# Spreading q and k by DMA and transposing them in 32x32 blocks on VectorE instead of TensorE

## The chip, the cores and the metric

One Trainium2 chip, one of its cores. The metric is the device time of one execution of the program in microseconds; lower is better. The profile is that of one execution, and its times are counted from the first instruction of the program (the start of the span).

## The reference

Chunked attention over eight batches of eight heads (576 rows, head size 64, chunks of 64 rows that attend only to themselves), and behind it a low-rank mix of the rows and a two-layer MLP with a residual:

```python
q_c = q.reshape(B, H, nc, chunk, D)        # B=8, H=8, S=576, D=64, chunk=64, nc=9
scores = scale * np.matmul(q_c, k_c.transpose(0, 1, 2, 4, 3))
scores = scores - np.max(scores, axis=-1, keepdims=True)
attn = np.exp(scores)
attn = attn / (np.sum(attn, axis=-1, keepdims=True) + 1e-09)
out = np.matmul(attn, v_c)
...
x = out.transpose(0, 2, 1, 3).reshape(B, S, H * D)   # 8 x 576 x 512
h = xt @ U @ V                                       # xt: x with the last two axes swapped, rank 32
u = x + h.transpose(0, 2, 1)
return u + np.maximum(u @ w_ch1, 0.0) @ w_ch2        # 512 -> 2048 -> 512
```

q, k, v are float32; U, V and the two weight matrices are float64 and are converted on the chip.

## The kernel before

The batches are worked in four pairs. A pair has 1152 rows, which are nine tiles of 128 rows; the tiles are named (pair, tile), (0,0) to (3,8). Three tiles make a group of 384 rows, on which the MLP works. Tile 4 of each pair straddles the two batches, so its loads come in two segments.

**Attention of one tile** (`attention_ops`). `load_qk` (L376) brings q and k of 128 rows with rows on partitions and heads and head elements along the free axis (256-byte pieces, one DMA each for q and k per segment, on SP's queue), `load_v` (L392) brings v in four DMAs. TensorE then turns q (`ps_qT`) and k (`ps_kT`): four 128x128 transposes each (L419) into a PSUM bank, which ScalarE copies to SBUF (`evacuate`, L433) as `qT_` and `kT_`. So head pairs stand side by side: heads 2h and 2h+1 fill the two halves of the partitions. The scores are 32 matmuls of 64x64 (L441), VectorE takes maxima and subtracts (L455, L459), ScalarE exponentiates (L463), TensorE transposes the result (`ps_eT`, L419 again), ScalarE copies it, 32 matmuls multiply with v (L472), VectorE scales into the tile's `x` (L490).

**MLP block** (one group, one f of 16): twelve matmuls of 384 columns `h` (L638), ScalarE's relu `hh` (L646), VectorE's remainder `hl` (L651), nine matmuls of 512 columns `o` (L664). TensorE sends the `o` matmuls of one block behind the `h` matmuls of the next, so relu and remainder have the time of one `h` and one `o` stretch. There are 192 blocks, 12 groups by 16.

**The weights** arrive during the first 190 us: for each f one `wraw` load (L325 and L329, 512 KB each, on SP), then a conversion from float64 that begins with ScalarE's L86 (`magnitude`), goes through six VectorE instructions and ends with ScalarE's L348 and VectorE's L351. ScalarE and VectorE run their instructions in order, relu and conversion on one queue.

**Order of the work.** All of pair 0's tiles ("early"), the weights, the first 32 MLP blocks (groups 0 and 1 of pair 0, both taking each f in turn as its weights arrive, `STRETCHES`) and tiles (1,0) and (1,1) (placed behind blocks 28 and 30, `GATES`) are `Op`s with an engine, a cost in us and the SBUF slots and PSUM banks that they take and free; `order()` simulates them and fixes the order on each engine. Behind that, pairs 1 to 3 run through `plan()`: during the 16 blocks of a group, the attention steps of coming tiles (`attend`), the low-rank steps and the mixing are laid between the MLP's matmuls at even distances, and the framework's scheduler settles the order. `attend` calls `ahead` at the start of a tile, which loads the next tile. q, k, v, their transposes and other temporaries of pairs 1 to 3 share eight `slot` buffers.

SP's queue issues, in order, nearly all DMAs: weights, q, k, v of pairs 1 to 3, and the stores of the output (L679).

Of the kernel before, what the change touches and what calls it, by code (L numbers as in the profile page):

```python
# [10 lines left out]
F32 = mybir.dt.float32  # L11
# [10 lines left out]
def kernel(  # L22
# [11 lines left out]
    nc = tc.nc  # L34
    B, H, S, D = q.shape
# [3 lines left out]
    DF, DM = moe_w_ch2.shape[0], moe_w_ch1.shape[0]  # L39
    P = 128  # L40
    C = 64
    D1 = D + 1
    HP = H // 2
    NCC = DM // P
    NF = DF // P
    NT = 2 * S // P
    GT = 3
    NEARLY = 9
    NX = 10
# [5 lines left out]
    NPAIR = B // 2  # L55
# [5 lines left out]
    work = ctx.enter_context(tc.tile_pool(name="work", bufs=1))  # L61
    psum = ctx.enter_context(tc.tile_pool(name="psum", bufs=8, space=bass.MemoryType.PSUM))

    dram = ctx.enter_context(tc.tile_pool(name="dram", bufs=1, space=bass.MemoryType.DRAM))
# [4 lines left out]
    def slot(dtype, name, shape=(P, 512)):  # L69
        return work.tile(list(shape), dtype, tag="slot", name=name, bufs=NS)  # L70
# [40 lines left out]
    rank = [0]  # L111
# [248 lines left out]
    def segments(pr, t):  # L360
        lo, hi = t * P, (t + 1) * P
        for e in range(2):
            a, z = max(lo, e * S), min(hi, (e + 1) * S)
            if a < z:
                yield a - lo, z - a, 2 * pr + e, a - e * S

    def early(pr, t):
        return pr == 0 and t < NEARLY

    loaded = {}  # L370
    begun = {}
    x_of = {}
    y_of = {}
    ut_of = {}

    def load_qk(pr, t):  # L376
        n = f"{pr}_{t}"
        if early(pr, t):
            words = wslot((4 * DM,), F32, "qkv_" + n)
            qn, kn = (words[:, z * DM : (z + 1) * DM].rearrange("p (h d) -> p h d", h=H) for z in range(2))  # L380
            vn = words[:, 2 * DM : 2 * DM + H * D1].rearrange("p (c a k) -> p c a k", c=2, k=D1)
        else:
            qn = slot(F32, "qn_" + n, (P, H, D))
            kn = slot(F32, "kn_" + n, (P, H, D))
            vn = slot(F32, "vn_" + n, (P, 2, HP, D1))
        nc.gpsimd.memset(vn[:, :, :, D:], 1.0)  # L386
        for r, m, b, s0 in segments(pr, t):
            nc.sync.dma_start(qn[r : r + m], q[b, :, s0 : s0 + m, :].rearrange("h s d -> s h d"))
            nc.sync.dma_start(kn[r : r + m], k[b, :, s0 : s0 + m, :].rearrange("h s d -> s h d"))
        loaded[pr, t] = qn, kn, vn  # L390

    def load_v(pr, t, behind=None):  # L392
        vn = loaded[pr, t][2]
        for c in range(2):
            b, s0 = divmod(t * P + c * C, S)
            b += 2 * pr
            for e in range(2):
                queue = nc.gpsimd if early(pr, t) else nc.sync
                d = queue.dma_start(
                    vn[e * C : (e + 1) * C, c, :, 0:D],  # L400
                    v[b, e::2, s0 : s0 + C, :].rearrange("h s d -> s h d"),
                )
                if behind is not None and c == e == 0:
                    sync = mybir.DependencyInfo(mybir.DependencyClass.Sync, mybir.DependencyReason.DATA)
                    tc.add_manual_dep(d.ins, behind.ins.name, sync, reason="q and k go first")

    def load(pr, t):
        load_qk(pr, t)
        load_v(pr, t)

    def attention_ops(pr, t, after=None):
        n = f"{pr}_{t}"
        st = {}
        mine = early(pr, t)

        def transpose(src, name):
            ps = st[name] = bank("ps_" + name + n)
            for j in range(4):
                o = nc.tensor.transpose(  # L419
                    ps[:, j * P : (j + 1) * P], src[:, j * P : (j + 1) * P], ident  # L420
                )
            if mine and name == "qT_":
                q_last[t] = o

        def evacuate(name):
            if name[0] == "e" or not mine:
                dst = slot(F32, name + n, (P, HP, P))
            elif name[0] == "q":
                st["qk"] = wslot((2, HP, P), F32, "qkT_" + n)
                dst = st["qk"][:, 0]  # L430
            else:
                dst = st["qk"][:, 1]
            nc.scalar.copy(dst.rearrange("p a b -> p (a b)"), st[name])  # L433
            st[name] = dst
# [51 lines left out]

        def scaled(e):
            if e == 0:
                st["x"] = work.tile([P, HP, 2, D], F32, tag="x", name="x_" + n, bufs=NX)
            nc.vector.tensor_mul(  # L490
                st["x"][:, :, e, :],
                st["av"][e][:, :, 0:D],
                st["sm"][:, e].unsqueeze(2).broadcast_to([P, HP, D]),
            )
            if e == 1:
                x_of[pr, t] = st["x"].rearrange("p a b k -> p (a b k)")

        src = lambda z: loaded[pr, t][z].rearrange("p h d -> p (h d)")
        flat = lambda: st["ex"].rearrange("p a b k -> p (a b k)")
        lq = Op("SP", 3.4, lambda: load_qk(pr, t), after, take="w" if mine else "slot slot slot", lat=1.6)  # L500
        tq = Op("PE", 0.55, lambda: transpose(src(0), "qT_"), lq, begun.get((pr, t - 2)), take="bank")
        lv = Op(
            "POOL" if mine else "SP",
            2.5,
# [2 lines left out]
            lat=2.2,  # L507
        )
        if mine:
            tqs[t], lvs[t] = tq, lv  # L510
        cq = Op("ACT", 0.58, lambda: evacuate("qT_"), tq, take="w" if mine else "slot", free="bank")
        tk = Op("PE", 0.55, lambda: transpose(src(1), "kT_"), lq, tq, take="bank")
        ck = Op("ACT", 0.58, lambda: evacuate("kT_"), tk, cq, take="" if mine else "slot", free="bank")
        sc = Op("PE", 0.62, scores, ck, take="bank bank", free="w" if mine else "slot slot slot slot")
        m0 = Op("DVE", 0.41, lambda: maximum(0), sc, take="slot mx")
        s0 = Op("DVE", 0.41, lambda: subtract(0), m0, free="bank")
        m1 = Op("DVE", 0.41, lambda: maximum(1), s0)
        s1 = Op("DVE", 0.41, lambda: subtract(1), m1, free="bank mx")
        ex = Op("ACT", 0.63, exp, s1)
        te = Op("PE", 0.55, lambda: transpose(flat(), "eT_"), ex, take="bank", free="slot")  # L520
        ce = Op("ACT", 0.58, lambda: evacuate("eT_"), te, take="slot", free="bank")
        av = Op("PE", 0.65, values, ce, lv, take="bank bank x", free="slot w" if mine else "slot slot")
        sm = Op("DVE", 0.5, sums, av, take="sm")
        x0 = Op("DVE", 0.415, lambda: scaled(0), sm, free="bank")
        x1 = Op("DVE", 0.415, lambda: scaled(1), x0, free="bank sm")
        begun[pr, t] = te
        return [[lq, lv], [tq, cq], [tk, ck], [sc, m0, s0, m1, s1, ex], [te, ce], [av, sm, x0, x1]]

    ybank = {}
    q_last, tqs, lvs, ahead = {}, {}, {}, {}  # L530
# [187 lines left out]
    WORK = "U T3 T4 T8 T5 T2 T1 T7 T0 T6 W0 P0 P1 V M0 M1 W1 W2 W3 W4 W5 W6 W7 W8 W9 W10 W11 W12 W13 W14 W15".split()  # L718
    STRETCHES = ((0, 0, 2), (1, 0, 2), (0, 2, 3), (1, 2, 3), (0, 3, 4), (1, 3, 4), (0, 4, 5), (1, 4, 5), (0, 5, 6), (1, 5, 6), (0, 6, 7), (1, 6, 7), (0, 7, 8), (1, 7, 8), (0, 8, 9), (1, 8, 9), (0, 9, 10), (1, 9, 10), (0, 10, 11), (1, 10, 11), (0, 11, 12), (1, 11, 12), (0, 12, 13), (1, 12, 13), (0, 13, 14), (1, 13, 14), (0, 14, 16), (1, 14, 16))
    GATES = (28, 30)  # L720
    BASE = 1000
    u_done = None
    v_done = []
# [5 lines left out]
    for item in WORK:  # L729
        rank[0] += 1  # L730
        begin = len(ops)
        z, i = item[0], int(item[1:] or 0)
# [21 lines left out]
        lvs[b].after.append(tqs[a])  # L754
    prev = None
    blocks = 0
    gates = dict(zip(GATES, range(len(GATES))))
    for g, f0, f1 in STRETCHES:
        for f in range(f0, f1):
            rank[0] = BASE  # L760
            prev = block_ops(0, g, f, f == 0, f == NF - 1, [*w_done[f], *mixed[g]], prev)
            blocks += 1
            if (g, f) == (0, NF - 1):
                last = prev
            if blocks in gates:
                rank[0] = 0
                attention_ops(1, gates[blocks], prev[0])
    assert blocks == 2 * NF
    rank[0] = 0
    for t in range(6, NT):  # L770
# [19 lines left out]
    manual.__exit__(None, None, None)  # L790


    tiles = [(pr, t) for pr in range(NPAIR) for t in range(NT)]
    pend = None

# [10 lines left out]
    def attend(ts):  # L806
        steps = []
        prev = None
        for key in ts:
            i = tiles.index(key)  # L810
            _, q, k, sc, et, av = attention_ops(*key)

            def ahead(i=i):
                if i + 1 < len(tiles) and tiles[i + 1] not in loaded:
                    load(*tiles[i + 1])

            steps += [ahead, step(*q)] + ([prev[0]] if prev else [])
            steps += [step(*k)] + ([prev[1]] if prev else []) + [step(*sc)]
            prev = step(*et), step(*av)
        return steps + (list(prev) if prev else [])  # L820
# [72 lines left out]
```

## Time and profile before

| | |
|---|---|
| runs | 1003.51, 1002.9, 1005.02 us; median 1003.51 us |
| span of the profiled execution | 1000.9 us; its page gives no other time of this execution |
| TensorE matmuls (PE) | 980.2 us busy, 98% |
| TensorE weight loads (PEld) | 854.2 us, 85% |
| VectorE (DVE) | 405.6 us, 41% |
| ScalarE (ACT) | 256.9 us, 26% |
| SP's DMA queue | 120320 packets, 52.18 MB, 20.5% of the time of 16 DMA engines |

In the profile a line such as `L419` is a line of the kernel; `<-` names what an instruction writes and reads; `x4` counts instructions. In rows of groups the numbers after the bar are busy time in us, mean time of one instruction in ns, and the idle time of the engine just before them with the instruction that ended it. Matmuls are pipelined and their ends are modelled: two that follow each other overlap, so the distance from start to start, not the duration, is what one adds to TensorE's time. In the timeline the first two columns are start and duration in us, several alike instructions are merged into one row, and square brackets give the idle time before. SP's rows are issues of DMAs.

### The profile page before, as it was taken

What the parts mean: (1) busy time and instruction counts of PE and PEld (TensorE: products, weight loads), DVE (VectorE), ACT (ScalarE), POOL (GpSimd) and SP (SyncE); (2) the same over time, 40 slices, a digit from 0 to 9 for tenths busy, and PEclk for the clock granted to TensorE, in tenths of its full rate; (3) what the DMA queues carried; (4) which work ended last, traced back from release to release, by engine and by line L of the source; (5) the groups of instructions that cost most, each with busy time, mean ns of one, the idle gap of its engine ahead of it and who ended that gap; (6) DMA issues with size and microseconds to landing.
All of it is one profiled execution on the core that took longest, in us unless ns stands there. A gap on an engine that the chain in (4) does not pass through costs nothing.

```text
span 1000.9 us, 16704 instructions
## 1 busy us (share of the span) xinstructions
PE 980.2 (98%) x7073; PEld 854.2 (85%) x7073; DVE 405.6 (41%) x813; ACT 256.9 (26%) x460; POOL 33.3 (3%) x89
## 2 busy tenths in 40 slices
PE   7799999999999999999999999999999999999998
PEld 4569999888888889888888898888888889989997
DVE  5789999652332434222333332322423233211211
ACT  4533433322322222221222221221322221111110
POOL 6500000000000000000000000000000000000000
PEclk8999999999999999999999999999999999999999
DMA  9962223152312102121120111021021000000000
GB/s 223 225 207 73 97 84 115 23 148 54 64 33 64 32 5 60 32 46 52 35 62 35 30 32 32 35 62 33 32 65 32 32 1 1 32 1 1 32 1 32
DMA packets 121914, 56.42 MB, mean 56 GB/s; under 512 B 106208, under 2 KB 114432, under 8 KB 121840
## 3 DMA queue, kind: packets, MB, share of 16 engines
q1 hardware_dynamic: 120320, 52.18, 20.5%
q0 software_dynamic: 1520, 3.17, 1.5%
q8 instruction: 56, 0.92, 0.4%
q14 instruction: 18, 0.15, 0.0%
HBM read 45.83 MB, written 9.51 MB: 55 GB/s over the span
## 4 chain that ended last, share of the span: by engine, by line
PE 71%; DVE 0%; ACT 0%; DVEq 0%; issue 0%; ACTq 0%
PE h L638 31%; PE o L664 31%; PE av L472 1%; PE sc L441 1%; PE ut L604 1%; PE ps_eT L419 1%; PE ps_qT L419 1%; PE ps_kT L419 1%; PE u L592 1%; PE y L552 1%; PE y L553 1%; DVE x L676 0%; DVE ex L459 0%; ACT ex L463 0%; DVEq L888 0%; DVE mx L455 0%
## 5 line engine op out<-in xcount | busy, mean ns | idle before, releaser
L638 PE MATMUL h<-uth,w 128*128 128x384 f32 x1536 | 425.2, 341 | 0.4 <-DVE x L490 0.3
L664 PE MATMUL o<-w,hh 128*128 128x512 f32 x1152 | 363.5, 403 | 0.0
L638 PEld LDWEIGHTS h<-uth,w 128*128 128x128 f32 x1536 | 281.3, 188 | 8.5 <-issue 0.8
L651 DVE SCALAR_TENSOR_TENSOR hl<-h,hh 128x384 fp32r<-128x384 f32 x192 | 106.7, 556 | 429.9 <-ACT hh L646 429.8
L638 PE MATMUL h<-utl,w 128*128 128x384 f32 x768 | 259.4, 338 | 0.0
L664 PEld LDWEIGHTS o<-w,hh 128*128 128x128 f32 x1152 | 207.7, 188 | 34.9
L646 ACT ACTIVATE hh<-h 128x384 fp32r<-128x384 f32 x192 | 94.3, 491 | 481.9 <-PE h L638 481.8
L664 PE MATMUL o<-w,hl 128*128 128x512 f32 x576 | 217.7, 395 | 0.0
L638 PEld LDWEIGHTS h<-utl,w 128*128 128x128 f32 x768 | 144.4, 188 | 6.3 <-DVE utl L617 0.3
L664 PEld LDWEIGHTS o<-w,hl 128*128 128x128 f32 x576 | 108.3, 188 | 24.8
L463 ACT ACTIVATE ex<-ex 128x512 f32<-128x512 f32 x36 | 22.7, 632 | 87.4 <-DVE ex L459 87.3
L455 DVE TENSOR_REDUCE mx<-sc 128x4 f32<-128x256 f32 x72 | 27.9, 417 | 31.7 <-PE sc L441 31.7
L598 DVE TENSOR_TENSOR x<-u,x 128x512 f32<-128x512 f32 x36 | 24.3, 684 | 27.1 <-PE u L592 26.8
L617 DVE TENSOR_TENSOR utl<-ut,uth 128x512 fp32r<-128x512 f32 x36 | 24.4, 688 | 20.3 <-ACT uth L612 20.3
L433 ACT COPY eT<-ps_eT 128x512 f32<-128x512 f32 x36 | 21.0, 587 | 37.4 <-PE ps_eT L419 37.2
L545 DVE TENSOR_TENSOR xl<-x,xh 128x512 fp32r<-128x512 f32 x30 | 20.5, 688 | 23.6 <-ACT xh L541 20.5
L612 ACT CAST uth<-ut 128x512 fp32r<-128x512 f32 x36 | 20.8, 588 | 31.6 <-PE ut L604 31.6
L459 DVE TENSOR_TENSOR ex<-sc,mx 128x256 f32<-128x256 f32 x72 | 27.9, 417 | 1.2 <-DVE mx L455 0.5
L490 DVE TENSOR_TENSOR x<-av,sm 128x256 f32<-128x256 f32 x72 | 27.2, 418 | 1.1
L386 POOL MEMSET vn<- 128x8 f32 x27 | 3.0, 113 | 698.9 <-PE y L553 171.1
L676 DVE TENSOR_TENSOR x<-o,x 128x512 f32<-128x512 f32 x36 | 23.3, 684 | 5.8 <-PE o L664 5.8
L348 ACT CAST w<-wroom 128x1024 fp32r<-128x1024 f32 (+1 forms) x19 | 17.1, 915 | 27.4 <-DVE wroom L101 27.4
(88 smaller groups left out, 606.6 us busy)
## 6 DMA issues: line engine op xcount, KB each, us to landing
wraw<-in_moe_w_ch_dram SPq DMA_DIRECT2D x32, 512.0 KB, 4.7
out_dram<-x SPq DMA_DIRECT2D x36, 256.0 KB, 2.1
vn<-in_v_dram SPq DMA_DIRECT2D x108, 64.0 KB, 2.8
qn<-in_q_dram SPq DMA_DIRECT2D x24, 256.0 KB, 3.4
kn<-in_k_dram SPq DMA_DIRECT2D x24, 256.0 KB, 4.0
qkv<-in_v_dram POOLq DMA_DIRECT2D x36, 64.0 KB, 6.6
qkv<-in_q_dram SPq DMA_DIRECT2D x8, 256.0 KB, 8.9
qkv<-in_k_dram SPq DMA_DIRECT2D x8, 256.0 KB, 8.0
```

The costliest lines, as they stand in the source:

```text
L419: o = nc.tensor.transpose(ps[:, j * P : (j + 1) * P], src[:, j * P : (j + 1) * P], ident)
L455: nc.vector.reduce_max(mx, st["sc"][e], axis=AX.X)
L459: nc.vector.tensor_sub(st["ex"][:, :, e, :], st["sc"][e], mx.unsqueeze(2).broadcast_to([P, HP, C]))
L463: nc.scalar.activation(exf, exf, AF.Exp, scale=SCALE)
L490: nc.vector.tensor_mul(st["x"][:, :, e, :], st["av"][e][:, :, 0:D], st["sm"][:, e].unsqueeze(2).broadcast_to([P, HP, D]),)
L598: nc.vector.tensor_add(x, st["u"], x)
L617: nc.vector.tensor_sub(ul[:, :, js], st["t"].rearrange("p (c t) -> p c t", c=NCC), uh[:, :, js])
L638: nc.tensor.matmul(ps[:, :GN], lhsT=w[:, z, cc], rhs=u[:, cc, :], start=(n == 0), stop=(n == 3 * NCC - 1))
L646: nc.scalar.activation(hh, ps[:, :GN], AF.Relu)
L651: nc.vector.scalar_tensor_tensor(hl, ps[:, :GN], 0.0, hh, op0=ALU.max, op1=ALU.subtract)
L664: nc.tensor.matmul(acc[g, j], lhsT=h[:, js], rhs=w2[f][:, z], start=(first and i == 0), stop=(final and i == 2),)
L676: nc.vector.tensor_add(x, ps, x)
```

## The change

For pairs 1 to 3 q and k are no longer turned by TensorE. Two steps take the place of the transposes:

1. `halve` copies, for one batch, one of q and k and one half g of the 64 head elements, all 576 rows and 8 heads to an HBM scratch `[576, 256]`: 576 x 8 pieces of 128 bytes, HBM to HBM, one DMA on SP. A pair needs eight of them. Pair 1's are eight `Op`s on SP, one with each of the blocks 4 to 11 of the planned part; those of a later pair are issued one or two per tile by `ahead` during the pair before.
2. `load_qk` fetches a tile from the scratch in 512-byte pieces, such that partition (2e+g)*32+j holds, for four blocks a of 32 rows, row 32a+j of four heads. That takes eight DMAs of 64 KB per tile instead of two of 256 KB (sixteen for tile 4). Then `squares`, one VectorE transpose of 32x32 blocks over 128x512 elements, gives `qT_` or `kT_` directly in SBUF.

Heads 0 to 3 now fill the lower half of the partitions and heads 4 to 7 the upper half (`heads`), for v and `x` too. Pair 0 keeps the old way.

```diff
+    halves = {}
+
+    def halve(b, z, g):
+        d = halves[b, z, g] = dram.tile([S, H * SQ], F32, name=f"half{'qk'[z]}_{b}_{g}")
+        nc.sync.dma_start(
+            d.rearrange("s (h i) -> s h i", h=H),
+            (q, k)[z][b, :, :, g * SQ : (g + 1) * SQ].rearrange("h s i -> s h i"),
+        )
+
+    def halvings(pr):
+        return [lambda b=b, z=z, g=g: halve(b, z, g) for b in (2 * pr, 2 * pr + 1) for z in range(2) for g in range(2)]
...
     def load_qk(pr, t):
...
-            qn = slot(F32, "qn_" + n, (P, H, D))
-            kn = slot(F32, "kn_" + n, (P, H, D))
+            qn = slot(F32, "qn_" + n, (P, P // SQ, P))
+            kn = slot(F32, "kn_" + n, (P, P // SQ, P))
             vn = slot(F32, "vn_" + n, (P, 2, HP, D1))
         nc.gpsimd.memset(vn[:, :, :, D:], 1.0)
+        if not early(pr, t):
+            for z, dst in enumerate((qn, kn)):
+                for r, m, b, s0 in segments(pr, t):
+                    for e in range(2):
+                        for g in range(2):
+                            x0 = (2 * e + g) * SQ
+                            nc.sync.dma_start(
+                                dst[x0 : x0 + SQ, r // SQ : (r + m) // SQ, :],
+                                halves[b, z, g][s0 : s0 + m, e * P : (e + 1) * P].rearrange(
+                                    "(a j) c -> j a c", j=SQ
+                                ),
+                            )
+            loaded[pr, t] = qn, kn, vn
+            return
...
+        def squares(z, name):
+            dst = slot(F32, name + n, (P, HP, P))
+            nc.vector.transpose(
+                dst.rearrange("p h (a j) -> p h a j", j=SQ),
+                loaded[pr, t][z].rearrange("p a (h i) -> p h a i", i=SQ),
+            )
+            st[name] = dst
...
+        lq = Op(
+            "SP", 3.4 if mine else 5.0, lambda: load_qk(pr, t), *after, take="w" if mine else "slot slot slot", lat=1.6
+        )
+        if mine:
+            tq = Op("PE", 0.55, lambda: transpose(src(0), "qT_"), lq, begun.get((pr, t - 2)), take="bank")
+        else:
+            tq = Op("DVE", 0.6, lambda: squares(0, "qT_"), lq, begun.get((pr, t - 2)), take="slot")
...
+        if mine:
+            cq = Op("ACT", 0.58, lambda: evacuate("qT_"), tq, take="w", free="bank")
+            tk = Op("PE", 0.55, lambda: transpose(src(1), "kT_"), lq, tq, take="bank")
+            ck = Op("ACT", 0.58, lambda: evacuate("kT_"), tk, cq, free="bank")
+            turned = [[tq, cq], [tk, ck]]
+        else:
+            ck = Op("DVE", 0.6, lambda: squares(1, "kT_"), tq, take="slot")
+            turned = [[tq], [ck]]
...
+    HALVES_FROM = 4
...
+            if blocks >= HALVES_FROM and second:
+                rank[0] = 0
+                in_halves = Op("SP", 0.6, second.pop(0), prev[0], lat=6.0)
             if blocks in gates:
+                assert not second
                 rank[0] = 0
-                attention_ops(1, gates[blocks], prev[0])
+                attention_ops(1, gates[blocks], prev[0], in_halves)
...
             def ahead(i=i):
                 if i + 1 < len(tiles) and tiles[i + 1] not in loaded:
                     load(*tiles[i + 1])
+                pr, t = tiles[i]
+                if pr + 1 < NPAIR:
+                    todo = to_halve.setdefault(pr + 1, halvings(pr + 1))
+                    for _ in range(-(-len(todo) // max(1, NT - 1 - t))):
+                        todo.pop(0)()
```

More of the change, by code (lines that the diff above doesn't have):

```diff
@@ L41 @@
     C = 64
+    SQ = 32
     D1 = D + 1
@@ L390, in load_qk, with heads @@
         loaded[pr, t] = qn, kn, vn
+    def heads(pr, t, e):
+        return slice(e, None, 2) if early(pr, t) else slice(e * HP, (e + 1) * HP)
     def load_v(pr, t, behind=None):
@@ L400, in load_v @@
                     vn[e * C : (e + 1) * C, c, :, 0:D],
-                    v[b, e::2, s0 : s0 + C, :].rearrange("h s d -> s h d"),
+                    v[b, heads(pr, t, e), s0 : s0 + C, :].rearrange("h s d -> s h d"),
                 )
@@ L409, in load, with attention_ops @@
         load_v(pr, t)
-    def attention_ops(pr, t, after=None):
+    def attention_ops(pr, t, *after):
         n = f"{pr}_{t}"
@@ L423, in transpose @@
                 q_last[t] = o
+        def squares(z, name):
[5 more added lines that the diff above has]
+            st[name] = dst
         def evacuate(name):
-            if name[0] == "e" or not mine:
+            if name[0] == "e":
                 dst = slot(F32, name + n, (P, HP, P))
@@ L488, in scaled @@
             if e == 0:
-                st["x"] = work.tile([P, HP, 2, D], F32, tag="x", name="x_" + n, bufs=NX)
+                st["x"] = work.tile([P, DM], F32, tag="x", name="x_" + n, bufs=NX)
+            by_head = st["x"].rearrange("p (h d) -> p h d", h=H)
             nc.vector.tensor_mul(
-                st["x"][:, :, e, :],
+                by_head[:, heads(pr, t, e), :],
                 st["av"][e][:, :, 0:D],
@@ L495, in scaled @@
             if e == 1:
-                x_of[pr, t] = st["x"].rearrange("p a b k -> p (a b k)")
-        src = lambda z: loaded[pr, t][z].rearrange("p h d -> p (h d)")
+                x_of[pr, t] = st["x"]
+        src = lambda z: loaded[pr, t][z].rearrange("p a b -> p (a b)")
         flat = lambda: st["ex"].rearrange("p a b k -> p (a b k)")
-        lq = Op("SP", 3.4, lambda: load_qk(pr, t), after, take="w" if mine else "slot slot slot", lat=1.6)
-        tq = Op("PE", 0.55, lambda: transpose(src(0), "qT_"), lq, begun.get((pr, t - 2)), take="bank")
+        lq = Op(
[5 more added lines that the diff above has]
+            tq = Op("DVE", 0.6, lambda: squares(0, "qT_"), lq, begun.get((pr, t - 2)), take="slot")
         lv = Op(
@@ L510, in attention_ops @@
             tqs[t], lvs[t] = tq, lv
-        cq = Op("ACT", 0.58, lambda: evacuate("qT_"), tq, take="w" if mine else "slot", free="bank")
-        tk = Op("PE", 0.55, lambda: transpose(src(1), "kT_"), lq, tq, take="bank")
-        ck = Op("ACT", 0.58, lambda: evacuate("kT_"), tk, cq, take="" if mine else "slot", free="bank")
+        if mine:
[6 more added lines that the diff above has]
+            turned = [[tq], [ck]]
         sc = Op("PE", 0.62, scores, ck, take="bank bank", free="w" if mine else "slot slot slot slot")
@@ L526, in attention_ops @@
         begun[pr, t] = te
-        return [[lq, lv], [tq, cq], [tk, ck], [sc, m0, s0, m1, s1, ex], [te, ce], [av, sm, x0, x1]]
+        return [[lq, lv], *turned, [sc, m0, s0, m1, s1, ex], [te, ce], [av, sm, x0, x1]]
     ybank = {}
@@ L756 @@
     blocks = 0
+    second = halvings(1)
     gates = dict(zip(GATES, range(len(GATES))))
@@ L790 @@
     manual.__exit__(None, None, None)
+    to_halve = {}
     tiles = [(pr, t) for pr in range(NPAIR) for t in range(NT)]
```

## The prediction

> **What bounds the kernel now.** I read the page first (shares, chain), then the same shares by stage.
>
> ```profile
> span 1000.9 us, 16704 instructions
> PE 980.2 (98%) x7073; PEld 854.2 (85%) x7073; DVE 405.6 (41%) x813; ACT 256.9 (26%) x460; POOL 33.3 (3%) x89
> ...
> PE 71%; DVE 0%; ACT 0%; DVEq 0%; issue 0%; ACTq 0%
> ```
> ```profile
> core 0: us, PE busy (x) PEld busy (x) DVE busy (x) ACT busy (x) POOL busy (x), PEclk, DMA share, GB/s
> 75.00:180.00 105.00, 105.00 (x525) 94.71 (x524) 99.92 (x131) 39.78 (x57) 0.00 (x0) 1.00 0.27 88
> 180.00:210.00 30.00, 28.21 (x236) 23.85 (x236) 19.33 (x39) 9.05 (x17) 0.34 (x3) 1.00 0.23 61
> 210.00:850.00 640.00, 639.45 (x4787) 563.39 (x4786) 204.49 (x468) 155.06 (x289) 2.59 (x23) 1.00 0.17 41
> 850.00:1000.00 150.00, 146.29 (x734) 131.60 (x732) 28.90 (x50) 18.40 (x37) 0.00 (x0) 1.00 0.04 16
> ```
>
> The chain names nothing but PE. By stage, PE is without a gap from 75 to 180 and for 639.45 of 640 us from 210 to 850, where 25 of the 27 changed tiles lie; VectorE has 435 us to spare there. Only from 75 to 180 is VectorE nearly full too (99.92 of 105, the weights' conversion). So a matmul taken out shortens the time by what it adds between its neighbours' starts, if nothing that takes its place comes late. That the MLP runs without other work laid in (850 to 1000, 146.29 of 150, the rest being the end) says that no wait inside a block appears when the blocks move together.
>
> **What is removed from TensorE.** 27 tiles by 8 transposes, 54 groups of four.
>
> ```profile
> L419 PE MATMUL ps_qT<-ident,qn 128*128 128x128 f32 x108 | 17.1, 274 | 0.0
> L419 PE MATMUL ps_kT<-ident,kn 128*128 128x128 f32 x108 | 16.2, 273 | 0.7 <-ACT qT L433 0.7
> L419 PEld LDWEIGHTS ps_qT<-ident,qn 128*128 128x128 f32 x108 | 13.4, 140 | 2.4
> L433 ACT COPY kT<-ps_kT 128x512 f32<-128x512 f32 x27 | 15.9, 588 | 17.3 <-PE ps_kT L419 16.5 <-DMA kn<-in_k_dram 0.8
> L433 ACT COPY qT<-ps_qT 128x512 f32<-128x512 f32 x27 | 15.8, 584 | 14.6 <-PE ps_qT L419 14.6
> ```
> ```profile
> 413.25 0.62 PE L664 MATMUL o<-w,hh 128*128 128x512 f32 x2
> 413.71 0.39 PE L664 MATMUL o<-w,hl 128*128 128x512 f32 x1
> ...
> 414.63 0.60 PE L419 MATMUL ps_qT<-ident,qn 128*128 128x128 f32 x4
> 414.99 0.70 PE L664 MATMUL o<-w,hh 128*128 128x512 f32 x2
> 415.52 0.39 PE L664 MATMUL o<-w,hl 128*128 128x512 f32 x1
> ```
>
> The timeline has one group between `o` matmuls. From its start to the next `o` 0.36 us pass (414.99 - 414.63), and the two `o` behind it take 0.53 us to the next start instead of 0.46 (415.52 - 414.99 against 413.71 - 413.25): 0.36 + 0.07 = 0.43 us a group, 0.108 us a transpose. 54 x 0.43 = 23.2 us. The busy sum 17.1 + 16.2 = 33.3 us counts overlapped tails and is too high; 216 weight loads of 0.140 us would be 30.2 us, which is the upper bound. I take 23.2.
>
> ScalarE loses 54 copies, 31.7 us; at 26% busy and outside the chain that is worth nothing by itself. The one wait between copy and transpose (0.7 us) is left out.
>
> **What VectorE gets.** 54 block transposes of 128x512. The trace has none. Nearest rows:
>
> ```profile
> L598 DVE TENSOR_TENSOR x<-u,x 128x512 f32<-128x512 f32 x36 | 24.3, 684 | 27.1 <-PE u L592 26.8
> L92 DVE TENSOR_SCALAR wroom<-wroom 128x512 f32<-128x512 f32 x6 | 2.5, 418 | 0.0
> ```
> ```profile
> 543.02 0.49 ACT L646 ACTIVATE hh<-h 128x384 fp32r<-128x384 f32 x1 [3.71 <-PE h L638]
> 543.55 0.56 DVE L651 SCALAR_TENSOR_TENSOR hl<-h,hh 128x384 fp32r<-128x384 f32 x1 [3.65 <-ACT hh L646]
> 547.47 0.60 PE L419 MATMUL ps_kT<-ident,kn 128*128 128x128 f32 x4
> ```
>
> One costs 0.42 to 0.69 us, twice that if strided blocks halve the rate; I take 0.69 (37 us in all, against 435 idle). What matters is `hl`, behind it in VectorE's queue: here `hl` is done at 544.11 and the next block's `h`, after which it is wanted, ends where the k transposes begin, at 547.47: 3.4 us of cover. A transpose of even 1.4 us fits; one that waits for its load longer than 3.4 us stalls TensorE. Cost taken: 0, bound by the loads' lateness below.
>
> **What SP and the DMA engines get.** First the halvings: 24 DMAs of 4608 pieces of 128 bytes, HBM to HBM, 288 pieces on each of 16 engines. The trace has no such packet. Two stretches that hold one sort of packet each (the queue's packets, MB, share of 16 engines): 520 to 545 us, 256-byte pieces of q, k, v; 110 to 160 us, eight weight DMAs.
>
> ```profile
> q1 hardware_dynamic: 1856, 0.46, 8.3%
> ```
> ```profile
> q1 hardware_dynamic: 2850, 4.70, 27.2%
> ```
>
> That is 0.083 x 25 x 16 / 1856 = 17.9 ns for some 250 bytes, and 0.272 x 50 x 16 / 2850 = 76 ns for 1649: 0.042 ns a byte, so 12.9 ns for 128. A halving then holds the engines 288 x 12.9 = 3.7 us; with 17.9 ns, 5.2 us; if read and write of a short piece each cost one such packet, 35.8 ns and 10.3 us. I take 5.2, since 17.9 is the nearest measured packet. The Trainium skill's page "DMA: Bandwidth & Descriptors", section Specifications, asks for transfers of 512 bytes or more for line rate and says that below it the engine does a read-modify-write; that speaks against 128-byte writes. Nothing in this trace shows it; by it the dear end would hold, and the time and the chance would be those of the second rival.
>
> What it costs depends on when. Pair 1's eight halvings are planned one per block; 525 matmuls in 105 us are 25 blocks of 4.2 us. The fourth block's `h` is done near 82 us (first `h` at 67.3, three blocks, 2.1 us), so the eight enter SP's queue from 82 to 111 us, among the weight loads:
>
> ```profile
> L638 PE MATMUL h<-uth,w x1536: 331/337/735, 67.3 to 991.8; 128*128 128x384 f32 x192
> ```
> ```profile
> 83.05 0.37 SPq L325 DMA_DIRECT2D wraw<-in_moe_w_ch_dram  x1
> ...
> 106.92 0.37 SPq L325 DMA_DIRECT2D wraw<-in_moe_w_ch_dram  x1
> ...
> 119.77 0.37 SPq L325 DMA_DIRECT2D wraw<-in_moe_w_ch_dram  x1
> ```
> ```profile
> DMA to landing us min/median/max: 4.6/4.9/12.2
> ```
> ```profile
> 140.63 0.49 ACT L646 ACTIVATE hh<-h 128x384 fp32r<-128x384 f32 x1 [2.99 <-PE h L638]
> 141.02 1.14 ACT L86 ACTIVATE wroom<-wraw 128x1024 f32<-128x1024 f32 x1
> ```
>
> These are f = 8, 10, 11 (9 lies between). A weight pair takes 27.2% of 50 us over four pairs, 3.4 us, and 5.3 us from first issue to landing (0.42 + 4.9 for the second DMA, L329). One queue serves in order, so f = 11 lands at 82 + 8T + 3 x 3.4 + 5.3 = 97.5 + 8T for halvings of T us, and ScalarE first touches it at 141.0. T = 5.2 gives 139: in time, by 2 us. Above T = 5.4 ScalarE waits, with the relu `hh` behind it in its queue, and TensorE stalls by nearly all of 8 x (T - 5.4). Cost taken: 0; bounds 0 and 8 x 4.9 = 39 us.
>
> The other 16 halvings have some 300 us a pair: 8 x 10.3 = 82 us even at the dear end.
>
> Second, the tile loads: 8 DMAs (16 for tile 4) instead of 2 (4). Packets halve to 512-byte ones, so engine time falls; issue grows. The tightest ordinary tile, (1,6):
>
> ```profile
> 259.96 0.54 SPq L388 DMA_DIRECT2D qn<-in_q_dram  x1
> ...
> 269.66 0.66 PE L419 MATMUL ps_qT<-ident,qn 128*128 128x128 f32 x4
> ```
> ```profile
> DMA to landing us min/median/max: 2.7/3.5/11.0
> ```
>
> Issue to use are 9.7 us, of which landing takes 3.5: 6.2 spare. Six more issues of 0.54 us leave 3.0. With a 5.2 us halving just ahead it is 2.2 late, still under `hl`'s 3.4. No tile of pairs 2 and 3 is as tight. For tile 4 and pair 1's crowd I take 1 us (bounds 0 and 6). A load that waits for its halving has only stores and later loads behind it on SP, and those have the same spare time. POOL's queue sees no change.
>
> **Sum.** 1000.9 - 23.2 + 1 = 978.7 of span. The page gives no time for this execution beyond its span; the median of the runs, 1003.51, lies 2.6 above it. 978.7 + 2.6 = 981.3, say 981.
>
> **Rivals.**
> - Partly late: T between 5.4 and 8 us (19 to 28 ns a packet), or several loads late. Loss 4 to 20 us beside the gain: 985 to 1001; at T = 7, 981 + 13 = 994. For it: only 2 us of room at T = 5.2. Against: 12.9 ns by the line through the two packets.
> - Slower: short HBM writes at the dear end. T = 10.3 makes f = 11 late by 39 us: 981 + 39 = 1020. It decides from 8 x (T - 5.4) = 23, T = 8.3 us or 29 ns a packet. For it: no short write to HBM is in this trace to exclude it. Against: reads of 256 bytes, scattered the same way, stream at 17.9 ns.
> - No change: TensorE's gap-free stream is merely refilled by waits of VectorE's in-order queue (block transposes waiting on loads, `hl` behind), 1003. It would need 23 us of stalls in 27 tiles, 0.9 each; 3.4 us of cover per tile speaks against.
> - More gain: weight loads, not matmuls, pace the transposes, 30 us: 974. The start distance of 0.108 us speaks against.
>
> **How the numbers follow.** Forecast (978 to 985) 0.60; partly late 0.20; slower 0.13; no change 0.04; more gain 0.03. So faster 0.83, same 0.04, slower 0.13, with 0.2% (2 us) as what a measurement of this kernel tells from no change. The range 976 to 1001 holds the forecast and the partly late case, 0.8; it reaches neither the 974 nor the slower case.
>
> **What would show it.** PE's instructions down by 216, and PE as full as before from 210 to 850, a stretch shorter by about 21 us (50 of 54 groups). VectorE up by 54 transposes of 0.4 to 0.7 us; ScalarE down by 31.7 us. L86 of f = 9 to 12 following L646 without idle time: if instead it waits for `wraw`, T is over 5.4. Packets of 128 bytes at 13 to 19 ns; over 29 ns I am wrong in sign. DVE transposes with idle time ended by a DMA and PE `o` waiting for `hl` would mean late loads.

## The result and the profile after

The changed kernel takes 1033.53 us (median of four runs, 1032.72 to 1035.81) against 1003.2 us: a ratio of 1.0311, 95% interval 1.0291 to 1.0331. It is 30 us slower, where 22 us less had been forecast. The profiled execution took 1035.81 us with a span of 1034.0 us, so 1.8 us lie around the span; 2.6 had been taken.

The page of the changed kernel, its shares, slices (PE, granted clock, DMA) and chain:

```profile
span 1034.0 us, 16517 instructions
PE 959.0 (93%) x6857; PEld 832.1 (80%) x6857; DVE 440.0 (43%) x867; ACT 227.4 (22%) x406; POOL 33.2 (3%) x89
...
PE   3028899999999999999999999999999999999998
...
PEclk7559999999999999999999999999999999999999
DMA  9999993231413101211212101211212000000000
...
PE 88%; SPq 6%; DMA 3%; DVE 1%; issue 1%; ACT 1%; DVEq 0%; ACTq 0%; POOLq 0%
```

TensorE has 216 instructions and 21 us of busy time less, as intended. But the second slice, 26 to 52 us, is empty on PE, the DMA engines are full for six slices (155 us), and the chain now has 6% on SP's queue. TensorE's waits for an early q load (in total, times, longest, in us), first in the kernel before and then in the changed one, and the first and last start of the changed kernel's `h` matmuls (L687 is the old L638) say how much that is:

```profile
PE ps_qT L419 <- DMA qkv<-in_q_dram: 0.5, 1, 0.5
```
```profile
PE ps_qT L449 <- DMA qkv<-in_q_dram: 59.8, 3, 58.5
```
```profile
L687 PE MATMUL h<-uth,w x1536: 331/337/739, 122.6 to 1024.7; 128*128 128x384 f32 x192
```

One wait of 58.5 us for an early q load of pair 0, and the first `h` at 122.6 us instead of 67.3: 55.3 us lost. From the first `h` to the end of the span it is 1034.0 - 122.6 = 911.4 us, before 1000.9 - 67.3 = 933.6: 22.2 us gained. 55.3 - 22.2 = 33.1 is the difference of the spans.

What stands in SP's queue at that time (timeline of SP; L381 is `halve`), and under it the second tile's q load in the kernel before:

```profile
1.76 0.43 SPq L415 DMA_DIRECT2D qkv<-in_q_dram  x1
2.24 0.58 SPq L416 DMA_DIRECT2D qkv<-in_k_dram  x1
2.87 9.26 SPq L381 DMA_DIRECT2D halfq<-in_q_dram  x2
...
55.86 7.20 SPq L381 DMA_DIRECT2D halfk<-in_k_dram  x2
63.11 3.71 SPq L415 DMA_DIRECT2D qkv<-in_q_dram  x1
...
73.01 0.62 SPq L326 DMA_DIRECT2D wraw<-in_moe_w_ch_dram  x1
```
```profile
2.86 3.23 SPq L388 DMA_DIRECT2D qkv<-in_q_dram  x1
```

Sixteen halvings, eight rows of two, run from 2.87 to 63.11 us, in front of the second tile's q and of the second weight pair. They are the halvings of pairs 2 and 3, which the program emits in `ahead`, hundreds of microseconds later. They read only inputs and write fresh scratch, so nothing ties them to that place, and the scheduler that settles the order behind the planned part put them at the head of the queue. By what rule it chose that place is not shown. Pair 1's eight, which are in the planned order, kept their place among the weights.

### The profile page after: what moved, and what is told of

It is laid out like the page before. It is cut to its first block, busy times and chain, and to the rows that moved or that the text cites. A ratio compares the mean times of both kernels' runs of the same rounds, so it can differ in the third digit from the quotient of the medians.

```text
span 1034.0 us, 16517 instructions
## 1 busy us (share of the span) xinstructions
PE 959.0 (93%) x6857; PEld 832.1 (80%) x6857; DVE 440.0 (43%) x867; ACT 227.4 (22%) x406; POOL 33.2 (3%) x89
## 4 chain that ended last, share of the span: by engine, by line
PE 88%; SPq 6%; DMA 3%; DVE 1%; issue 1%; ACT 1%; DVEq 0%; ACTq 0%; POOLq 0%
PE h L687 39%; PE o L713 39%; SPq L381 6%; DMA qkv<-in_v_dram 2%; PE sc L479 2%; PE av L510 2%; PE ut L653 2%; PE ps_eT L449 1%; PE u L641 1%; PE y L601 1%; PE y L602 1%; PE y L608 1%; DMA qkv<-in_k_dram 0%; SPq L415 0%; ACT ex L501 0%
## 5 line engine op out<-in xcount | busy, mean ns | idle before, releaser
L687 PE MATMUL h<-uth,w 128*128 128x384 f32 x1536 | 423.9, 341 | 0.0
L713 PE MATMUL o<-w,hh 128*128 128x512 f32 x1152 | 357.5, 399 | 0.1
L687 PEld LDWEIGHTS h<-uth,w 128*128 128x128 f32 x1536 | 281.2, 188 | 8.2 <-issue 0.2
L687 PE MATMUL h<-utl,w 128*128 128x384 f32 x768 | 259.4, 338 | 0.0
L713 PEld LDWEIGHTS o<-w,hh 128*128 128x128 f32 x1152 | 210.8, 188 | 37.9 <-ACT hh L695 1.3
L687 PEld LDWEIGHTS h<-utl,w 128*128 128x128 f32 x768 | 144.3, 188 | 6.1 <-DVE utl L666 0.3
L449 PE MATMUL ps_qT<-ident,qkv 128*128 128x128 f32 x36 | 6.6, 313 | 59.8 <-DMA qkv<-in_q_dram 59.8
L449 PEld LDWEIGHTS ps_qT<-ident,qkv 128*128 128x128 f32 x36 | 4.6, 160 | 62.5 <-DMA qkv<-in_q_dram 59.0
L457 DVE STREAM_TRANSPOSE qT<-qn 128x512 f32<-128x512 f32 x27 | 19.1, 709 | 31.8 <-PE y L601 16.1
```

Source lines behind the costliest of these rows:

```text
L449: o = nc.tensor.transpose(ps[:, j * P : (j + 1) * P], src[:, j * P : (j + 1) * P], ident)
L687: nc.tensor.matmul(ps[:, :GN], lhsT=w[:, z, cc], rhs=u[:, cc, :], start=(n == 0), stop=(n == 3 * NCC - 1))
L713: nc.tensor.matmul(acc[g, j], lhsT=h[:, js], rhs=w2[f][:, z], start=(first and i == 0), stop=(final and i == 2),)
```

## The experiments

The theory (A, place): all of the loss is those sixteen DMAs in front of the early loads. The rival (B, price): the scratch traffic, the many small tile loads or VectorE's waits cost as much wherever they lie.

**Holding the sixteen halvings back.** Each one of pairs 2 and 3 waits for the last VectorE block transpose emitted before it:

```diff
...
+        if b >= 4:
+            sync = mybir.DependencyInfo(mybir.DependencyClass.Sync, mybir.DependencyReason.DATA)
+            tc.add_manual_dep(o.ins, turned_last[-1].ins.name, sync, reason="not before its time")
...
```

> The changed kernel, with each of the 16 halvings of pairs 2 and 3 made to wait for the last VectorE block transpose emitted before it; nothing else differs. Theory A (place): these 16 DMAs had nothing to wait for and stood at the head of SP's queue, so they cost the 55 us by which the first h came later (122.6 against 67.3 us); behind that point the change gains 22 us (911.4 against 933.6). Then the first h is back at 67 to 70 us, the span behind it stays near 911 us, and the time is 979 to 983 us. Rival B (price): the spread traffic, the tile loads or VectorE's waits cost as much wherever the halvings stand; then the time stays above 1015 us.

Measured: 981.19 us (980.18 to 983.12), ratio 0.9778, interval 0.9759 to 0.9796. Its first `h`, and its halvings' first and last issues:

```profile
L693 PE MATMUL h<-uth,w x1536: 331/337/736, 67.4 to 970.8; 128*128 128x384 f32 x192
```
```profile
L383 SPq DMA_DIRECT2D halfq<-in_q_dram x12: 549/574/10381, 52.1 to 445.3; - x12
L383 SPq DMA_DIRECT2D halfk<-in_k_dram x12: 549/570/5407, 67.6 to 499.3; - x12
```

The first `h` is back at 67.4, and 980.2 - 67.4 = 912.8 us lie behind it. One edge in the dependencies of each of the sixteen DMAs is worth 52 us in all. Theory A stands, B falls.

**The halvings alone, unread, in the kernel before.** `halve` and its calls in `ahead` were added to the kernel before and nothing else, once for pairs 2 and 3 (sixteen), once for pair 2 (eight).

> The kernel before, which turns q and k on TensorE, with the 16 halvings of pairs 2 and 3 added as DMAs whose result nobody reads. Theory A: they stand behind the second early load on SP, hold the 16 DMA engines 16 x 3.6 us, the first h comes 55 us later, and the time is 1003 + 55 = 1058 us (1053 to 1063). Rival B: the loss of the changed kernel came from its use of the scratch, and idle DMA engines take the copies in passing: 1003 to 1010 us.

> The kernel before with only pair 2's eight unread halvings. Theory A: half of the delay, the first h 26 to 29 us later, 1029 to 1033 us. A rival within A: the start has slack, so that the first few halvings are free; then the delay is clearly under half of that with sixteen, below 20 us.

Measured: 1056.92 us with sixteen (ratio 1.0533, 1.0511 to 1.0556) and 1026.71 us with eight (1.023, 1.0214 to 1.0245). TensorE's longest wait and the first `h`, sixteen and then eight:

```profile
PE ps_qT L431 <- DMA qkv<-in_q_dram: 60.9, 3, 58.5
```
```profile
L650 PE MATMUL h<-uth,w x1536: 331/337/739, 120.2 to 1044.7; 128*128 128x384 f32 x192
```
```profile
PE ps_qT L431 <- DMA qkv<-in_q_dram: 30.8, 3, 29.8
```
```profile
L650 PE MATMUL h<-uth,w x1536: 331/337/737, 92.0 to 1016.4; 128*128 128x384 f32 x192
```

The wait is 58.5 and 29.8 us, 3.7 us a halving. The first `h` comes 52.9 and 24.7 us later, 5 to 6 us less than the wait: the start has that much slack once. The rival of the second expectation, a delay below 20 us, did not come. The 1026.71 lies 2 us under the range given, because the slack was not counted.

**The transposes left out, nothing in their place.** In the kernel before, `qT_` and `kT_` of pairs 1 to 3 are the loaded tiles themselves.

> The kernel before, which leaves out the transposes of q and k in pairs 1 to 3 and their copies (the scores there are of unturned rows); loads as before. It is the change's gain with nothing in its place. By the start distances of TensorE, 54 x 0.43 = 23.2 us: 980 us (978 to 982). Rivals: weight loads set the pace of the transposes, 30 us, 973; or the gap is refilled by other waits, over 990.

Measured: 978.13 us, ratio 0.9747 (0.9722 to 0.9772), 25.7 us under the kernel before. The span behind the first `h` (68.1) is 908.8 us, 24.8 less than before. So the removed work is worth 25 us, between the 23.2 worked out and the weight loads' 30; with it goes the need for two of the shared buffers per tile, which was not separated. The held kernel gains 20.8 behind its first `h` (912.8 against 933.6).

**A second copy of each held halving.**

> The held kernel with each of the 16 halvings of pairs 2 and 3 followed by a second copy into a scratch that nobody reads. Theory A (a halving costs nothing where the queue has nothing urgent behind it): the same as held, a ratio of 0.976 to 0.980 to the kernel before, 979 to 984 us. Rival: SP's in-order queue makes tile loads late, each extra halving costs its 3.6 us in part: over 16 x 1 us more, 997 us and up.

Measured: 1001.3 us, ratio 0.998 (0.9962 to 0.9997): the expectation missed, and the rival's number came. The windows (busy times from PE on, then granted clock, DMA share and GB/s), first of the held, then of the doubled kernel, from the start of the 34th block to shortly before that of the 50th:

```profile
214.00:296.00 82.00, 80.13 (x691) 69.13 (x690) 35.75 (x84) 19.03 (x35) 0.68 (x6) 1.00 0.64 121
```
```profile
214.00:314.90 100.90, 83.07 (x691) 71.85 (x690) 35.76 (x84) 19.01 (x35) 0.67 (x6) 0.92 0.84 142
```

All of the loss is there: this stretch is 18.9 us longer, the whole span 18.8 (999.0 against 980.2), and behind it the two kernels run alike (the 96 blocks from the 64th on take 463.2 us in the held kernel and 463.1 in the doubled one). In it pair 1's first tiles follow closely, and pair 2's halvings lie between their loads. SP, VectorE, ScalarE and TensorE of the doubled kernel:

```profile
266.03 0.61 SPq L383 DMA_DIRECT2D halfq<-in_q_dram  x1
266.69 3.23 SPq L391 DMA_DIRECT2D againq<-in_q_dram  x1
270.03 3.73 SPq L383 DMA_DIRECT2D halfq<-in_q_dram  x1
273.80 3.78 SPq L391 DMA_DIRECT2D againq<-in_q_dram  x1
277.99 3.18 SPq L440 DMA_DIRECT2D vn<-in_v_dram  x1
281.29 1.96 SPq L417 DMA_DIRECT2D qn<-halfq  x4
```
```profile
285.24 0.71 DVE L468 STREAM_TRANSPOSE qT<-qn 128x512 f32<-128x512 f32 x1 [14.69 <-DMA qn<-halfq]
```
```profile
285.99 0.58 ACT L483 COPY eT<-ps_eT 128x512 f32<-128x512 f32 x1 [16.03 <-DVE qT L468]
```
```profile
286.67 1.29 PE L522 MATMUL av<-vn,eT 64*64 64x65 f32 x32 [12.68 <-issue]
```

Four copies stand in front of a q load, and VectorE's transpose waits 14.69 us for it. ScalarE's copy `eT` of the tile before waits for that transpose, 16.03 us; the copy does not read what the transpose writes, so the tie is probably one of the shared buffers. TensorE's `av` reads `eT`, and TensorE stands for 12.68 us (the view names no releaser for it). The next block's `h` then takes 4.1 us instead of 2.1: from 288 to 292 us the granted clock was 0.50, in the held kernel 1.00 around that place.

**The same doubling, with pair 2's halvings moved behind that stretch.** They are issued two each at tiles 5 to 8 of pair 1:

```diff
...
-                    for _ in range(-(-len(todo) // max(1, NT - 1 - t))):
+                    for _ in range(2 * (t > 4) if pr == 1 else -(-len(todo) // max(1, NT - 1 - t))):
...
```

> As held_late, and each of the 16 halvings of pairs 2 and 3 followed by a second, unread copy, as in the doubled run that came to 1001 us. If those 20 us were paid only between 214 and 296 us, where pair 2's copies lay between pair 1's tile loads, then with the copies moved behind that stretch the time is 980 to 986 us. Rival: 16 more copies cost their 20 us wherever they lie: 995 to 1003 us.

> The held kernel with pair 2's eight halvings issued two each at tiles 5 to 8 of pair 1, instead of two, two and one each from tile 2 on; so SP's queue has only tile loads while pair 1's first tiles follow each other closely. If the halvings cost the held kernel its small rest there (from 212 to 295 us it takes 1.8 us more than the kernel that leaves the transposes out), 978 to 981 us, ratio 0.974 to 0.977. Rival: the rest is the longer issue of the tile loads or VectorE's own time; then the same as held, 0.976 to 0.980.

> The held kernel once more, on the same chip as the two others, to tell a difference of 1 or 2 us: 979 to 983 us.

Measured: doubled and moved 985.82 us (ratio 0.9829, 0.9805 to 0.9853), moved alone 981.37 us (0.9787, 0.9768 to 0.9807), held once more 982.89 us (0.98, 0.978 to 0.982). Moving the copies brings back 15 of the 20 us, so most of their price was their place. Of the 3 to 5 us left over the three undoubled measurements, the traces show some 1.4 from the 45th to the 48th block (14.7 us instead of 13.3); the rest is not explained. In the times, moving the undoubled halvings gives no difference that these runs can tell. In the traces it does: from the start of the relu of the 37th block to that of the 45th the two held executions take 47.2 and 47.3 us, held and moved 45.8, and the kernel without transposes 45.6. Held, moved or not, beats both the kernel before and the changed one.

**Pair 1's halvings at three times the price.** In the held kernel each of the eight that lie among the weight loads is followed by two unread copies.

> The held kernel with pair 1's eight halvings, which lie among the weight loads from 52 to 94 us, each followed by two unread copies: a halving price of 3 x 3.6 = 11 us, the dear end of the prediction. By adding up SP's queue, 24 copies of 3.6 us and four weight pairs of 3.4 us from 52 us on, the ninth weight pair lands at about 155 us instead of the 124.2 us at which ScalarE first reads it, 31 us late; ScalarE waits with the relu behind it: 1005 to 1014 us. Rival: the weights' lead in the slots or the remainder of the blocks' cover takes it up: under 990 us.

Measured: 1020.38 us, ratio 1.018 (1.0155 to 1.0206), 39 us over the held kernel, more than expected. ScalarE's L87 (the old L86) and the waits of TensorE:

```profile
114.50 1.13 ACT L87 ACTIVATE wroom<-wraw 128x1024 f32<-128x1024 f32 x1 [6.70 <-DMA wraw<-in_moe_w_ch_dram]
138.84 1.12 ACT L87 ACTIVATE wroom<-wraw 128x1024 f32<-128x1024 f32 x1 [19.64 <-DMA wraw<-in_moe_w_ch_dram]
163.26 1.12 ACT L87 ACTIVATE wroom<-wraw 128x1024 f32<-128x1024 f32 x1 [16.13 <-DMA wraw<-in_moe_w_ch_dram]
```
```profile
PE o L725 <- ACT hh L707: 32.7, 3, 16.1
```

The mechanism is the one worked out: ScalarE waits for weights, the relu behind it in its queue comes late, and TensorE waits for the relu. The tenth weight pair (f = 9, which the expectation calls the ninth) is first read at 163.3 instead of 124.2 us, 39 late and not 31; the queue, still full of early loads at 52 us, started on the copies later than the sum had it (its first three took 16.7 us to issue, not 11).

**No scratch at all.** Thirty-two DMAs per tile fetch 128-byte pieces from the inputs:

```diff
...
+                            for a in range(m // SQ):
+                                nc.sync.dma_start(
+                                    dst[x0 : x0 + SQ, r // SQ + a, :].rearrange("j (h i) -> j h i", i=SQ),
+                                    (q, k)[z][
+                                        b, heads(pr, t, e), s0 + a * SQ : s0 + (a + 1) * SQ, g * SQ : (g + 1) * SQ
+                                    ].rearrange("h j i -> j h i"),
+                                )
...
```

> The changed kernel without the scratch: each tile's q and k come from the inputs straight into the layout that VectorE turns, in 128-byte pieces, 32 DMAs of 16 KB per tile instead of 8 (no halvings at all). Theory A: no DMA is free to go to the head of the queue, so the first h comes at 67 to 70 us and TensorE's gain stands; at some 0.55 us an issue, 32 take SP 18 us per tile, less than the 25 us that a tile has on the mean, but more than the 7 to 13 us between the first tiles of pair 1: 983 to 995 us. Rivals: SP is fast enough, 979 to 982; or VectorE's wait for the loads stalls every tile, over 1003.

Measured: 1029.88 us, ratio 1.0281 (1.0249 to 1.0313). The first `h` is at 65.0 us, but around 200 to 260 us SP does nothing but issue; the second view is what VectorE's `kT` transposes wait for k loads:

```profile
221.17 8.87 SPq L407 DMA_DIRECT2D qn<-in_q_dram  x16
230.14 7.49 SPq L407 DMA_DIRECT2D kn<-in_k_dram  x16
237.68 2.58 SPq L430 DMA_DIRECT2D vn<-in_v_dram  x4
240.68 7.56 SPq L407 DMA_DIRECT2D qn<-in_q_dram  x16
```
```profile
DVE kT L458 <- DMA kn<-in_k_dram: 35.6, 11, 6.9
```

A tile takes SP 19 us, more than pair 1's first tiles leave it. Neither the range nor the rival "every tile" was right. From the relu of the 32nd block to that of the 45th, where pair 1's first tiles lie, this kernel takes 123.3 us and the held one 73.4; behind that the two differ by 0.9 us (692.7 and 691.9 to the last relu).

## Why the prediction was wrong, step by step

- **The step that failed** is the sentence on the sixteen halvings of pairs 2 and 3, that they "have some 300 us a pair", at no cost. It took the place in the program's text for the place in the queue. The runs showed them from 2.87 to 63.11 us, for 58.5 us of TensorE's wait and 55.3 us of delay; held to their place, the same DMAs leave 981.19 us, against 981 forecast. None of the rivals named this mechanism: those that made the kernel lose by its halvings took the order of the queue as given and asked what one costs. That "slower" was among them is luck, since its price, over 8.3 us a halving, was not found. And that the held kernel hits the 981 is partly luck too: more was removed than summed (25 against 23.2 us), and more was added (3 against 1).
- **What is removed**: 23.2 us were summed; leaving the transposes out is worth 25. The start distances were a good measure, the busy sum (33.3) and the weight loads (30.2) were too high.
- **The price of a halving** was put at 5.2 us, between 3.7 and 10.3. Sixteen in 60.2 us are 3.8 us, or 13 ns a packet: the line through the two measured packets (12.9 ns) was right as the pace of a stream, and the nearest packet too dear. (The stretch of weight DMAs held packets of several sizes, not one sort; its 1649 bytes are a mean.) By the measure of the line itself, the time that packets take, one took 15.0 ns (116.7% of 52 us on 16 engines for 64602 packets, 8 to 60 us): they overlap. The Trainium skill's page "DMA: Bandwidth & Descriptors", section Specifications, says that below 512 bytes the engine does a read-modify-write. By time no extra price is to be seen here, as the 128-byte pieces written to HBM lie near that line; but its lower point, 250 bytes, is itself under 512, so a price that all short packets pay would not show.
- **Pair 1's halvings** cost nothing at their own price, as said: the relu of the 29th block starts at 191.1 us in the kernel before and in the held one. But the same error is in their placing. They were placed by block times, from 82 us on; SP did not wait for these blocks and issued them from 52 us in the held kernel. That gave more room than the 2 us worked out. At three times the price the stall came, by ScalarE's queue.
- **VectorE**: 0.69 us was taken for one transpose; the changed kernel shows

```profile
L457 DVE STREAM_TRANSPOSE qT<-qn x27: 702/711/715, 244.9 to 824.6; 128x512 f32<-128x512 f32 x27
L457 DVE STREAM_TRANSPOSE kT<-kn x27: 669/701/714, 247.4 to 831.2; 128x512 f32<-128x512 f32 x27
```

  and no cost of its own; from 258 us on PE of the changed kernel is as full as that of the kernel before (627.31 of 628 us, windows):

```profile
258.00:886.00 628.00, 627.31 (x4645) 548.60 (x4644) 240.32 (x525) 128.51 (x241) 2.70 (x24) 1.00 0.15 43
```

- **The tile loads**: 1 us was allowed in pair 1's crowd, with 6 as the bound. The held kernel lies 3 us above the one without transposes. By the starts of the blocks' relus in the traces, 1.6 us of it arise from the 37th to the 45th block and 2.0 behind it. The first part is nearly all the halvings', since it shrinks to some 0.1 us where they lie elsewhere: moved (45.8 us), and in the changed kernel (45.8), whose sixteen went ahead of everything. The second part is not theirs, since the changed kernel, which has none there, takes the same 691.9 us from the 45th block's relu to the last as the held one, against 689.9 without transposes. Whether the tile loads, VectorE's transposes or the buffers make these 2 us was not settled.

## What to carry to other kernels

A DMA that reads only inputs and writes fresh memory has no place of its own: before costing it, look for what holds it where the program's text has it, and give it an edge where nothing does. On an in-order queue the price of a transfer is what stands behind it: the same copies cost 3.7 us each in front of the first loads, nothing among loads with a lead (three times as many there cost 39 us), and some 20 us for eight more of them between loads that were just in time. Test such a thing by adding the transfers alone, unread, to the kernel before.

## What the runs showed of the hardware

Copies of 128-byte pieces from HBM to HBM ran at 13 ns a piece on each of 16 engines in a stream, no dearer than the line through reads of 250 and 1649 bytes (averages). SP's issue of such a copy, when it stood behind another one, lasted about as long as the copy: 14 of the 16 issues in the head of the changed kernel took 3.3 to 4.1 us. The first of a row behind a weight pair took 0.55 us, in the kernel with the tripled copies even at 134.1 us, when the DMA share was 1.21. So a long copy holds the issuing queue and not only the engines. Whether the same copies on another queue would have delayed the loads as much was not tried.
